# Attention by 64 query rows of both heads, and the last expert block by tiles, in an attention and mixture-of-experts kernel

## The chip, the core and the metric

The kernel runs on one core of a Trainium2 chip. The core has the matrix engine PE (its weight loads are listed as PEld, beside the products), the vector engine DVE, ACT, POOL and the queue engine SP; 16 DMA engines move data. The metric is the device time of one execution in microseconds; kernels are compared by the median of their runs.

## The reference

Attention with 8 batches, 8 heads, 576 positions and head size 64. A query sees itself and the 127 keys before it, with a slope per head. Its result is the input `x` (4608 rows of 512) of a layer with 8 experts of which each row takes two.

```python
scores = scale * np.matmul(q, k.transpose(0, 1, 3, 2))
mask = (rel >= 0) & (rel < window)          # rel = query - key, window = 128
scores = np.where(mask, scores + bias[None], -1000000000.0)
attn = np.exp(scores - np.max(scores, axis=-1, keepdims=True))
attn = attn / (np.sum(attn, axis=-1, keepdims=True) + 1e-09)
...
noisy_logits = x @ w_gate + np.log1p(np.exp(x @ w_noise)) * noise
top2 = np.argpartition(-noisy_logits, 2, axis=1)[:, :2]
...
h = np.maximum(x[mask] @ w1[e], 0.0)
out[mask] += top2_w[mask, k, None] * (h @ w2[e])
```

## The kernel before

**Order.** Nothing is scheduled by the compiler: `attention_moe` describes the work as strands (generators), and the class `Order` plays them in its own model of the engines. Each step has a rank; a free engine takes the waiting step of lowest rank, and the instructions are written out in that order. The ranks are sums of the table of constants at the head of the file (`LOAD`, `STAGE`, `LATE` and others). Buffers and PSUM banks are rings; a strand waits in the model for a free one. What runs on each engine is therefore a fixed list, and the chip's semaphores make it wait where the data isn't there.

**Attention.** A pair is two heads of one batch, 32 in all. `unit` (L559) takes a pair's 576 queries in three groups: blocks of 128 queries (0, 1), (2, 3) and the last 64 of both heads together. `scores` (L470) multiplies, in float32, each block with up to 256 keys, one head on the upper 64 rows of the array and the other on the lower 64 (L480), each head into a bank of its own; the last 64 queries use all 128 rows (L473). `sb` (L412) is one entry that holds both banks. `top` (L492, rows named L498) adds the bias on DVE and takes the row minimum, `soft` (L501, L505) the exponentials on ACT, `trans` (L511, L517) transposes on PE in squares of 128 (16 a pair), `evac` copies them to SBUF on ACT or DVE, and `weigh` (L530, L538 and L544) multiplies with V, the two heads side by side on 64 columns of the array each. `rows` and `gate` then turn the result to rows and compute the gate; `route` (L754) ranks the rows of a batch by expert with 20 products of 8 columns (`ranks`, L774).

**Experts.** Weights and activations are split into two float16 halves, so every product is made of three. `ups` (L1202, L1199 in the rows) makes the hidden layer in chunks of 128, `middle` the activation on ACT and DVE, `downs` (L1254, L1246 in the rows) adds each chunk's part to all tiles of 128 rows of the block, and `result` (L1316) scales a tile and adds it to the output with an indirect DMA on POOL. Blocks of the first two experts run as soon as a share of the batches is routed, among the attention; the others follow. `weight` (L1083) loads a weight chunk and finds its largest value (L1090) on DVE. SP issues the loads in the planned order.

Of the kernel before, what the change touches and what calls it, by code (L numbers as in the profile page):

```python
# [22 lines left out]
NQ = 5  # L23
NP = H // 2
QW = 512 + 128
GROUPS = ((0, 1), (2, 3), (4,))
# [17 lines left out]
ZERO = 157.5  # L44
LOAD = 136.5
VALUES = 180.6
GATE = (-31.6, -127.8)
ROUTE = 0
SCATTER = (-98.7, -1299.1, 241.8)
FFN0, FFN1 = 110.0, 337.8  # L50
WEIGHTS = ((17.1, 19.6), (205.3, 22.3))
SEQUENCE = ((0, 0), (0, 1), (1, 0), (1, 1), (0, 2), (1, 2), (0, 3), (1, 3))
TOKENS = -340.5
STAGE = (-252.5, -341.8, -103.3, -45.5, 28.3, -118.2, 102.9, -69.8)
MIDDLE = -39.8
RESULT = -351.1
WEIGHTS_LATE = 141.4
SOON = 126.4
LISTED = (-148.6, 389.0)
BIG, PARTS = 198.5, 29.3  # L60
TIGHT = (1, 5, 7)
LATE = (-250.4, 168.7, 5.2, 55.5, 53.4, 102.3, -331.2, -32.4, -14.5, 0.7, 30.3, 27.9)
# [24 lines left out]
class Op:  # L87


    def __init__(self, on, emit, join=True):  # L90
        self.on, self.emit, self.join, self.taken = on, emit, join, False
# [16 lines left out]
class Order:  # L108
# [3 lines left out]
    def __init__(self):  # L112
# [4 lines left out]
        self.work = {}  # L117
# [49 lines left out]

    def dispatch(self, e):
        if self.busy[e] > self.now:
            return  # L170
        while self.queue[e]:
            _, _, us, what, strand = heapq.heappop(self.queue[e])
            if what.taken:
                continue
# [9 lines left out]
            return  # L184
# [25 lines left out]
class Block:  # L210


    def __init__(self, e, s0, n, rows, rings):
        self.e, self.s0, self.n, self.rows, self.rings = e, s0, n, rows, rings
        self.last = self.flip = False
# [8 lines left out]
def attention_moe(ctx: ExitStack, tc: tile.TileContext, qk_, v, w_gate, w_noise, noise, w12,  # L224
# [19 lines left out]
    def pe(us, rank, emit, join=True):  # L244
        return Op((("PE", us, rank),), emit, join)
# [30 lines left out]
    pr = ring(ap_, 3, [128, 2, 2, 256], F32, "p")  # L276
    nmr = ring(ap_, 3, [128, 2, 2], F32, "nm")
    ptr = [ring(ap_, 2, [128, 2, 7, 128], F32, "pT"), ring(ap_, 1, [128, 2, 128], F32, "pTl")]
    xur = [ring(ap_, 2, [128, NP, 512], F32, "xu"), ring(ap_, 2, [128, NP, 64], F32, "xul")]
    denr = ring(ap_, 3, [128, NQ, H], F32, "den")  # L280
    xr = ring(ap_, 4, [128, DM], F32, "x")
    ltr = ring(ap_, 1, [128, 4, H, 16], F32, "lt")
    gtr = ring(ap_, 2, [128, 512], F32, "gt")

    PAIRS = B * NP
    units = [(k, g) for k in range(PAIRS) for g in range(len(GROUPS))]
# [9 lines left out]
    relc, m1 = scratch[0][:, 0:256], scratch[0][:, 256:512]  # L296
# [35 lines left out]
    def masks():  # L332
# [14 lines left out]
        for g in range(NP):  # L347
            for h in (2 * g, 2 * g + 1):
                yield either(0.56, 0.37, -20 + 5 * g, LATE[9], lambda e, h=h: bias_of(e, h))
            mark(biased[g])  # L350
# [1230 lines left out]
```

## Time and profile before

| | |
|---|---|
| median of 3 runs | 1095.0 us (1094.45 to 1097.28) |
| profiled execution | 1096.31 us, span 1094.5 us |
| PE, DVE, ACT, POOL busy | 96%, 64%, 43%, 33% of the span |
| mean granted PE clock | 0.996 |
| DMA | 145.61 MB |

The span goes from the first to the last instruction; the execution's time has 1.8 us beyond it. A product's record includes its latency, so groups of products overlap and a busy PE isn't one at its peak: how long a group holds the engine is read from its start to the next group's start. An idle time is given with the instruction that ended it.

### The profile page before, as it was taken

How to read it: one execution, taken by the hardware profiler on the slowest of the kernel's cores; microseconds unless marked ns; L12 is line 12 of the kernel's file. 1: busy time of each engine (PE TensorE's matmuls, PEld its weight loads, DVE VectorE, ACT ScalarE, POOL GpSimd, SP SyncE). 2: the span in 40 equal slices, each digit the busy share in tenths (PEclk: the TensorE clock that was granted, in tenths of full speed). 3: DMA queues.
4: the chain of work that ended last, by engine and by line, in shares of the span. 5: the costliest groups of instructions: out<-in, count | busy, mean ns of one | idle time of the engine just before them, and what ended most of it. 6: DMA issues, size and time to landing. Idle time of an engine off the chain costs nothing. (4 is left out here: it accounts for less than half of the span.)

```text
span 1094.5 us, 20083 instructions
## 1 busy us (share of the span) xinstructions
PE 1051.7 (96%) x7158; PEld 645.5 (59%) x7158; DVE 700.4 (64%) x2431; ACT 468.4 (43%) x1221; POOL 357.6 (33%) x464
## 2 busy tenths in 40 slices
PE   7888899999999999999999999999999999999995
PEld 5656666766676666564456446645754574564453
DVE  6999989968847889544469845925673582432110
ACT  7887777757622325222135423513352351321221
POOL 1377741444332423142113333203232231321211
PEclk9999999999999999999999999999999999999998
DMA  9757786534423687347495458557753753752212
GB/s 347 287 167 257 254 264 228 158 112 125 75 75 85 99 232 146 73 93 177 143 182 101 79 119 167 66 148 130 123 101 91 151 83 64 111 82 38 28 20 40
DMA packets 130085, 145.61 MB, mean 133 GB/s; under 512 B 90416, under 2 KB 91264, under 8 KB 129984
## 3 DMA queue, kind: packets, MB, share of 16 engines
q1 hardware_dynamic: 112464, 104.97, 34.6%
q0 software_dynamic: 17520, 39.34, 21.5%
q8 instruction: 57, 0.93, 0.4%
q14 instruction: 44, 0.36, 0.1%
HBM read 83.94 MB, written 40.91 MB: 114 GB/s over the span
## 5 line engine op out<-in xcount | busy, mean ns | idle before, releaser
L1199 PEld LDWEIGHTS <-held 128*128 128x128 f16 x2424 | 233.9, 98 | 127.7 <-issue 4.3
L1199 PE MATMUL bank<-bx,held 128*128 128x512 f16 (+7 forms) x1752 | 301.6, 324 | 0.1
L1235 DVE SCALAR_TENSOR_TENSOR bhl<-bank,bhh 128x384 f16<-128x384 f32 (+7 forms) x160 | 87.8, 549 | 284.0 <-ACT bhh L1220 279.4
L1326 POOL DMA_INDIRECT out_dram<-yo,ix x62 | 102.3, 1651 | 414.2 <-ACT yo L263 393.7
L1220 ACT ACTIVATE bhh<-bank 128x384 f16<-128x384 f32 (+7 forms) x144 | 70.1, 487 | 353.4 <-PE bank L1199 343.7
L1246 PE MATMUL bank<-held,bhh 128*128 128x512 f16 x728 | 216.5, 379 | 0.5 <-ACT bhh L1220 0.5
L505 ACT ACTIVATE p<-p,nm 128x256 f32<-128x256 f32 (+2 forms) x288 | 134.1, 472 | 19.7 <-DVE nm L498 19.4
L1246 PE MATMUL bank<-held,bhl 128*128 128x512 f16 x364 | 138.0, 379 | 0.0
L1246 PEld LDWEIGHTS <-bhh 128*128 128x128 f16 x800 | 78.6, 98 | 84.2 <-ACT bhh L1220 0.7
L498 DVE CUSTOM_DVE_ANT_0 p<-bank,bias 128x256 f32<-128x256 f32 (+2 forms) x288 | 95.2, 380 | 11.9 <-PE bank L480 9.0
L480 PE MATMUL bank<-qk 64*128 64x256 f32 (+1 forms) x512 | 73.7, 389 | 19.4 <-DVE nm L498 15.8
L517 PE MATMUL bank<-ident,p 128*128 128x128 f32 x512 | 78.5, 285 | 4.2 <-DVE l L846 1.0
L263 ACT ACTIVATE xt<-xg,fit 128x512 f16<-128x512 f32 (+5 forms) x77 | 55.3, 719 | 60.2 <-DVE fit L1167 52.8
L1154 POOL DMA_INDIRECT xg<-xs_dram,ix x62 | 65.4, 1056 | 45.3 <-DVE xt L1182 12.8
L1090 DVE TENSOR_REDUCE wam<-held 128x2 f32<-128x1024 f32 x60 | 71.9, 1211 | 5.3 <-DMA held<-in_w_dram 5.3
L1199 PE MATMUL bank<-ax,held 128*128 128x256 f16 (+1 forms) x672 | 75.0, 266 | 0.3 <-DVE ahl L1235 0.3
L517 PEld LDWEIGHTS bank<-ident,p 128*128 128x128 f32 x512 | 57.4, 143 | 23.5 <-ACT p L505 7.3
L480 PEld LDWEIGHTS bank<-qk 64*128 64x128 f32 x512 | 45.1, 194 | 38.7 <-DVE nm L498 26.1
L1121 DVE SCALAR_TENSOR_TENSOR held<-held,wsc,held 128x512 f16<-128x512 f32 x92 | 67.2, 771 | 0.0
L1246 PEld LDWEIGHTS <-bhl 128*128 128x128 f16 (+1 forms) x400 | 39.4, 98 | 47.1 <-DVE bhl L1235 0.3
L263 ACT ACTIVATE held<-held,wsc 128x512 f16<-128x512 f32 x92 | 61.6, 714 | 12.9 <-DVE held L1121 8.9
L1246 PE MATMUL bank<-held,ahh 128*128 128x512 f16 x224 | 67.1, 381 | 0.0
(238 smaller groups left out, 1499.4 us busy)
## 6 DMA issues: line engine op xcount, KB each, us to landing
held<-in_w_dram SPq DMA_DIRECT2D x60, 512.0 KB
qk<-in_qk_dram SPq DMA_DIRECT2D x31, 608.0 KB
vraw<-in_v_dram SPq DMA_DIRECT2D x16, 640.0 KB
out_dram<-xg SPq DMA_DIRECT2D x10, 1024.0 KB
xs_dram<-x SPq DMA_DIRECT2D x32, 256.0 KB
spare<-in_w_dram SPq DMA_DIRECT2D x4, 512.0 KB
xs_dram<-x SPq DMA_DIRECT2D x8, 128.0 KB
xs_dram<-xg SPq DMA_DIRECT2D x1, 1024.0 KB
```

The lines of the kernel that those rows point to most:

```text
L263: nc.scalar.activation(o, i, AF.Copy, **kw)
L480: nc.tensor.matmul(s[h][:, o:o + c], qk[half, i * 128:i * 128 + 128], qk[half, QW + k0:QW + k0 + c], start=True, stop=True)
L498: nc.vector.tensor_tensor_reduce(out=p[:, z, h, 0:c], in0=s[h][:, o:o + c], in1=bv, scale=-0.125, scalar=3.0e38, op0=OP.add, op1=OP.min, a ...
L505: nc.scalar.activation(pv, pv, AF.Exp, bias=nm[:, z, h:h + 1], scale=-1.0, accum_out=den[:, i, 2 * g + h:2 * g + h + 1])
L517: nc.tensor.transpose(t[:, z], p[:, h, a:a + 128], ident)
L1090: yield dve(1.13, rank + (BIG if e >= EARLY else 0), lambda: nc.vector.tensor_reduce(wam[:, e % 2, :, f], t.rearrange("p (z c) -> p z c", ...
L1121: nc.vector.scalar_tensor_tensor(lo, t, sc, hi, op0=OP.mult, op1=OP.subtract)
L1199: nc.tensor.matmul(t[:, 0:blk.n], wp[:, c], blk.x[:, x + c, 0:blk.n], start=c == 0 and z == 0, stop=c == 3 and z == 2)
L1220: nc.scalar.activation(o, i, AF.Relu)
L1235: yield dve(0.07 + c * 0.00104, rank - MIDDLE, lambda: nc.vector.scalar_tensor_tensor(hl[:, 0:c], t[:, 0:c], 0.0, hh[:, 0:c], op0=OP.max, ...
L1246: nc.tensor.matmul(blk.y[j][0:r], h[:, cs], wp, start=f == 0 and m == 0, stop=f == 7 and m == 2)
L1326: ins = nc.gpsimd.indirect_dma_start(out=out, out_offset=bass.IndirectOffsetOnAxis(ap=blk.ix[0:r, j:j + 1], axis=0), in_=t[0:r], in_offset ...
```

## The change

- **Scores.** A group is now 128 queries of both heads as two sub-blocks of 64: the array's 128 columns hold 64 queries of one head and 64 of the other, its 128 rows both heads' 64 dimensions, with zeros in between (laid out by the host in `qk`, so a pair's load has 1728 columns instead of 1216). A sub-block meets at most 192 keys. There are five groups a pair and nine products of 64, 128 and seven times 192 columns. A group writes one bank; `sb` has two entries.
- **Transposes.** Two sub-blocks lie next to each other in `p` so that their halves share a square: 13 a pair instead of 16.
- **Weighing V.** Per sub-block and head one product of full height (128 keys) and one of half height (64 keys), each of 64 columns; even sub-blocks to one bank, odd ones to another.
- **Ranks.** Six products of 48 to 8 columns a batch.
- **Last block.** Its hidden layer is kept whole; then one tile takes all its eight chunks, then the other. The last tile's scaling is cut in two halves for ACT and DVE, and POOL drains before the first of the block's scatters.
- **Order.** The planner prefers PE steps of the shape that the array has; the table of constants is new; expert 1's weight loads have an earliest time.

```diff
-QW = 512 + 128
-GROUPS = ((0, 1), (2, 3), (4,))
+NS, SUB = S // 64, 64
+QW = NS * 128
...
-PACE = (36.1, 5.5)
-AHEAD = -83.9
+PACE = (33.7, 5.5)
+HOLD = (-38.7, 125.2)
...
+STAY, TURN = -100.7, 0.13
...
+    def take(self, e):
+        q = self.queue[e]
+        while q:
+            if e == "PE":
+                x = min(q, key=lambda x: (x[0] + (STAY if x[3].shape != self.shape else 0.0), x[1]))
+                q.remove(x)
+                heapq.heapify(q)
+            else:
+                x = heapq.heappop(q)
+            if not x[3].taken:
+                return x[2:]
+        return None
+    def cost(self, e, us, what):
+        if e == "PE":
+            us, self.shape = us + (TURN if what.shape != self.shape else 0.0), what.shape
+        return us
...
-    pr = ring(ap_, 3, [128, 2, 2, 256], F32, "p")
...
+    pr = ring(ap_, 6, [128, 384], F32, "p")
...
-    sb, tb, ob, yb = Ring([bank[0:2]]), Ring([*bank[2:4], bank[7]]), Ring([bank[4], bank[6]]), Ring([])
+    sb, tb, ob, yb = Ring(bank[0:2]), Ring([*bank[2:4], bank[7]]), Ring([bank[4], bank[6]]), Ring([])
...
             t = yield (vraw, rank)
+            yield begun
...
-        if blocks == (4,):
-            nc.tensor.matmul(s[0][:, 0:192], qk[:, 512:QW], qk[:, QW + S - 192:QW + S], start=True, stop=True)
-            return
-        for z, i in enumerate(blocks):
-            k0, c = (i - 1) * 128 if i else 0, width(i)
-            o = place_of(blocks, z)
-            for h in range(2):
-                half = slice(h * D, h * D + D)
-                nc.tensor.matmul(s[h][:, o:o + c], qk[half, i * 128:i * 128 + 128], qk[half, QW + k0:QW + k0 + c],
...
+    def subs(i):
+        return range(2 * i, min(2 * i + 2, NS))
+    def width(j):
+        return min(64 * j + 64, 192)
+    def place(j):
+        return (192, 384)[j % 2] - width(j)
...
+        for j in subs(i):
+            c, k1 = width(j), QW + 64 * j + 64
+            nc.tensor.matmul(s[:, j % 2 * 256:j % 2 * 256 + c], qk[:, j * 128:j * 128 + 128], qk[:, k1 - c:k1],
+                             start=True, stop=True)
...
+    def turns(i):
+        return range(i == 0, 3 - (i == 4))
...
+        for z, a in enumerate(turns(i)):
+            nc.tensor.transpose(t[:, z * 128:z * 128 + 128], p[:, a * 128:a * 128 + 128], ident)
...
-        for z in range(4):
-            c = min(256, 512 - 128 * z)
+        def part_of(o, j, rows, block, slot, first_, last):
             for h in range(2):
                 half, hh = slice(h * D, h * D + D), (k % 2 * 2 + h) * D
-                nc.tensor.matmul(o[half, z * 128:z * 128 + c], t[:, z, hh:hh + D],
-                                 pt.rearrange("p h s c -> p h (s c)")[:, h, 2 * z * 128:2 * z * 128 + c],
-                                 start=z == 0, stop=z == 3, skip_group_check=True)
-        for z in range(2):
-            for h in range(2):
-                half, hh = slice(h * D, h * D + D), (k % 2 * 2 + h) * D
-                nc.tensor.matmul(ol[half], t[:, 3 + z, hh:hh + D], ptl[:, z, half], start=z == 0, stop=z == 1)
+                nc.tensor.matmul(o[half, j // 2 * SUB:j // 2 * SUB + SUB], t[rows, block, hh:hh + D], pt[rows, slot, half],
+                                 start=first_, stop=last, skip_group_check=True)
+        for a in range(4):
+            part_of(odd, 2 * a + 1, slice(0, 128), a, 3 * a + 1, a == 0, False)
+            part_of(even, 2 * a + 2, slice(0, 128), a, 3 * a + 2, a == 0, False)
+        for i in range(NQ):
+            if 0 < i < 4:
+                part_of(odd, 2 * i + 1, slice(64, 128), i - 1, 3 * i, False, i == 3)
+            part_of(even, 2 * i, slice(0, 64), i, 3 * i, False, i == 4)
...
         def ranks():
-            for i in range(NQ):
-                nc.tensor.matmul(rp[:, i], before, both_[:, i], start=True, stop=i == 0)
-                for j in range(i):
-                    nc.tensor.matmul(rp[:, i], ones, both_[:, j], start=False, stop=j == i - 1)
             for j in range(NQ):
-                nc.tensor.matmul(rp[:, NQ], ones, both_[:, j], start=j == 0, stop=j == NQ - 1)
+                nc.tensor.matmul(rp[:, j + 1:], ones, both_[:, j:j + 1].to_broadcast([128, NQ - j, E]), start=j == 0,
+                                 stop=False, skip_group_check=True)
+            nc.tensor.matmul(rp, before, both_, start=False, stop=True, skip_group_check=True)
...
     def weight(e, f, t, rank):
+        if e < EARLY and order.now < HOLD[e]:
+            yield Pad(HOLD[e])
...
+        if blk.final:
+            if not f:
+                blk.hx = yield (blk.rings["x"], rank)
+                mark(blk.hid)
+            yield blk.hid
+            hh, hl = (blk.hx[:, f, z * 256:z * 256 + c] for z in range(2))
...
+    def last_downs(blk, rank):
+        blk.y = []
+        for j, r in blk.tiles:
+            t = yield (yb, rank)
+            blk.y.append(t)
+            for f in range(8):
+                yield blk.h[f][0]
+                ev = chunks[blk.e, f]
+                yield ev[1]
+                end = yield pe(0.655, rank, lambda: mm2(blk, f, j, r, ev[2]), False)
+            spawn(result(blk, j, r, rank - RESULT, end))
...
+            if blk.final and not j:
+                nc.gpsimd.drain()
...
-        yield either(0.57, 0.66, rank, LATE[7], lambda e: copy(e, t[0:r], y[0:r], scale=gw))
+        if blk.final and j == len(blk.tiles) - 1:
+            both = Event(2)
+            for z, (on, us) in enumerate((("ACT", 0.33), ("DVE", 0.36))):
+                spawn(half(on, us, rank, t[0:r, z * 256:z * 256 + 256], y[0:r, z * 256:z * 256 + 256], gw, both))
+            yield both
+        else:
+            yield either(0.57, 0.66, rank, LATE[7], lambda e: copy(e, t[0:r], y[0:r], scale=gw))
...
-    qk[..., 0:512], qk[..., QW:] = q[..., 0:512], k
+    qk[..., QW:] = k
     for h in range(2):
-        qk[:, h, :, 512 + 64 * h:512 + 64 * h + 64] = q[:, h, :, 512:]
+        for j in range(NS):
+            qk[:, h, :, j * 128 + h * 64:j * 128 + h * 64 + 64] = q[:, h, :, 64 * j:64 * j + 64]
```

On PE, at the third pair of heads, before: `qk_79` and `qk_80` hold queries and keys of two pairs, bank_66 and bank_67 are the score banks, `p` the exponentials and `pT` their transposes, `vraw` V.

```order
L480 MATMUL bank_66<-qk_79 128x256
L480 MATMUL bank_67<-qk_79 128x256
L538 MATMUL bank_70<-pT_90,vraw_82 64x256 x6
L538 MATMUL bank_70<-pT_90,vraw_82 64x128 x2
L544 MATMUL bank_71<-pTl_92,vraw_82 64x64 x4
L473 MATMUL bank_66<-qk_79 128x192
L517 MATMUL bank_73<-ident,p_84 128x128 x2
L517 MATMUL bank_68<-ident,p_84 128x128 x4
L480 MATMUL bank_66<-qk_80 128x128
L480 MATMUL bank_67<-qk_80 128x128
```

After, at the same place:

```order
L523 MATMUL bank_73<-ident,p_89 128x128 x2
L502 MATMUL bank_66<-qk_79 128x192 x2
L502 MATMUL bank_67<-qk_79 128x192
L523 MATMUL bank_69<-ident,p_84 128x128 x3
L502 MATMUL bank_66<-qk_80 128x64
L502 MATMUL bank_66<-qk_80 128x128
L523 MATMUL bank_73<-ident,p_85 128x128 x3
L537 MATMUL bank_68<-pT_96,vraw_82 64x64 x2
L537 MATMUL bank_70<-pT_96,vraw_82 64x64 x2
```

Scores go one bank at a time between transposes, and V is weighed in short pieces that alternate between two banks.

On ACT, at the end of the last block, before (`bhh` is the upper half of a hidden chunk, `yo` a scaled tile, bank_69 and bank_70 the two tiles' sums):

```order
L1220 ACTIVATE bhh_4677<-bank_66 128x240
L1220 ACTIVATE bhh_4678<-bank_71 128x240
L1220 ACTIVATE bhh_4679<-bank_67 128x240
L1220 ACTIVATE bhh_4677<-bank_66 128x240
L263 ACTIVATE yo_197<-bank_69,gw_194 128x512
L263 ACTIVATE yo_4691<-bank_70,gw_194 112x512
```

After (`bx_5121` holds all hidden chunks, bank_73 and bank_72 are the tiles' sums):

```order
L1219 ACTIVATE bx_5121<-bank_66 128x240
L1219 ACTIVATE bx_5121<-bank_71 128x240
L1219 ACTIVATE bx_5121<-bank_67 128x240
L283 ACTIVATE yo_203<-bank_73,gw_198 128x512
L283 ACTIVATE yo_5136<-bank_72,gw_198 112x256
```

The second tile's scaling has half its columns on ACT; on PE the eight chunks' products of bank_73 now stand ahead of all those of bank_72, where before each chunk fed both tiles in turn.

On SP, where loads of the first pairs and of the first experts' weights (`held`) are issued, before:

```order
L1086 DMA held_111<-in_w_dram 128x1024
L1086 DMA held_112<-in_w_dram 128x1024
L388 DMA wgn<-in_w_gate_dram 64x4x8
L434 DMA qk_78<-in_qk_dram 128x1216
L1086 DMA held_113<-in_w_dram 128x1024
L1086 DMA held_114<-in_w_dram 128x1024
L1086 DMA held_115<-in_w_dram 128x1024
L1086 DMA held_116<-in_w_dram 128x1024
L1086 DMA held_117<-in_w_dram 128x1024
L1086 DMA held_118<-in_w_dram 128x1024
L1086 DMA held_119<-in_w_dram 128x1024
L1086 DMA held_120<-in_w_dram 128x1024
```

After:

```order
L1087 DMA held_119<-in_w_dram 128x1024
L1087 DMA held_120<-in_w_dram 128x1024
L452 DMA qk_78<-in_qk_dram 128x1728
L408 DMA wgn<-in_w_gate_dram 64x4x8
L452 DMA qk_79<-in_qk_dram 128x1728
L463 DMA vraw_83<-in_v_dram 128x1280
L452 DMA qk_80<-in_qk_dram 128x1728
L452 DMA qk_81<-in_qk_dram 128x1728
L408 DMA wgn<-in_w_noise_dram 64x4x8
L452 DMA qk_78<-in_qk_dram 128x1728
L463 DMA vraw_82<-in_v_dram 128x1280
L408 DMA wgn<-in_w_noise_dram 64x4x8
```

Behind the first weights there were ten more; now six loads of pairs and V and two small ones follow, and expert 1's weights come later.

## Rows read from the trace of the kernel before

**Rows 1.** Page part 1: busy us of each engine (share), x instructions.

```profile
PE 1051.7 (96%) x7158; PEld 645.5 (59%) x7158; DVE 700.4 (64%) x2431; ACT 468.4 (43%) x1221; POOL 357.6 (33%) x464
```

**Rows 2.** Windows by stage: start:end, length, engines' busy us, clock, DMA share, GB/s.

```profile
0.00:27.40 27.40, 21.34 (x137) 14.97 (x138) 18.60 (x72) 20.68 (x70) 3.20 (x23) 1.00 0.93 348
27.40:136.80 109.40, 94.96 (x830) 67.02 (x829) 105.74 (x390) 86.77 (x292) 70.76 (x73) 1.00 0.71 241
136.80:301.00 164.20, 158.41 (x1473) 113.22 (x1474) 142.01 (x728) 118.14 (x423) 66.73 (x122) 1.00 0.55 160
301.00:465.00 164.00, 160.16 (x1208) 104.98 (x1205) 121.24 (x432) 50.97 (x105) 51.30 (x67) 1.00 0.55 119
465.00:1079.20 614.20, 613.76 (x3502) 343.58 (x3500) 312.37 (x810) 190.17 (x329) 162.56 (x178) 1.00 0.54 103
1079.20:1094.50 15.30, 3.10 (x20) 1.69 (x18) 0.41 (x1) 1.71 (x3) 3.08 (x3) 0.71 0.25 33
```

**Rows 3.** Waits of PE's weight loads: waited for, us in total, times, longest.

```profile
PEld bank L480 <- DVE nm L498: 26.1, 34, 1.8
...
PEld bank L517 <- ACT p L505: 7.3, 21, 1.3
...
PEld bank L473 <- DVE nm L498: 3.1, 5, 0.9
```

**Rows 4.** Timeline of PE, one pair: start, us, line, tiles, xcount, idle before.

```profile
111.97 0.93 PE L480 MATMUL bank<-qk 64*128 64x128 f32 x8 [0.74 <-DVE nm L498]
112.86 2.19 PE L517 MATMUL bank<-ident,p 128*128 128x128 f32 x16
115.53 1.47 PE L480 MATMUL bank<-qk 64*128 64x256 f32 x8 [0.47 <-DVE nm L498]
116.94 1.73 PE L538 MATMUL bank<-pT,vraw 128*64 128x256 f32 x16
118.50 0.40 PE L544 MATMUL bank<-pTl,vraw 128*64 128x64 f32 x8
118.83 0.44 PE L517 MATMUL bank<-ident,p 128*128 128x128 f32 x2
119.58 0.59 PE L473 MATMUL bank<-qk 128*128 128x192 f32 x2 [0.31 <-DVE nm L498]
120.01 0.60 PE L517 MATMUL bank<-ident,p 128*128 128x128 f32 x4
```

**Rows 5.** Timeline of PE, scores whose banks were free, and the group behind.

```profile
281.54 1.14 PE L480 MATMUL bank<-qk 64*128 64x256 f32 x8
282.60 0.66 PE L517 MATMUL bank<-ident,p 128*128 128x128 f32 x4
```

**Rows 6.** Timeline of PE, ranking of one batch: its first product, the group behind.

```profile
102.85 0.20 PE L776 MATMUL bank<-both,before 128*128 128x8 bf16 x2
...
103.37 1.98 PE L517 MATMUL bank<-ident,p 128*128 128x128 f32 x14
```

**Rows 7.** Groups on DVE, 27.4 to 301 us: xcount, busy us, mean ns, idle before.

```profile
L498 DVE CUSTOM_DVE_ANT_0 p<-bank,bias 128x256 f32<-128x256 f32 x175 | 64.5, 418 | 3.6 <-PE bank L480 3.3 <-issue 0.2
...
L498 DVE CUSTOM_DVE_ANT_0 p<-bank,bias 128x128 f32<-128x128 f32 x58 | 14.1, 279 | 1.2 <-PE bank L480 1.1
L1090 DVE TENSOR_REDUCE wam<-held 128x2 f32<-128x1024 f32 x11 | 13.2, 1212 | 0.0
...
L498 DVE CUSTOM_DVE_ANT_0 p<-bank,bias 128x192 f32<-128x192 f32 x30 | 10.4, 348 | 2.4 <-PE bank L517 2.2
```

**Rows 8.** Timeline of all engines, the end of the last block.

```profile
1082.16 1.33 ACT L263 ACTIVATE yo<-bank,gw 128x512 f32<-128x512 f32 x2 [0.92 <-PE bank L1246]
...
1082.39 0.38 PE L1246 MATMUL bank<-held,bhl 128*112 128x512 f16 x1
1083.12 1.55 POOL L1326 DMA_INDIRECT out_dram<-yo,ix  x1 [14.48 <-ACT yo L263]
...
1084.97 1.50 POOL L1326 DMA_INDIRECT out_dram<-yo,ix  x1 [0.27 <-issue]
```

More of the change, by code (lines that the diff above doesn't have):

```diff
@@ L116, in __init__ @@
         self.alive = 0
-        self.work = {}
+        self.work, self.shape = {}, 0
     def at(self, time, call):
@@ L170, in dispatch @@
             return
[L171 to L174, printed above, removed]
+        x = self.take(e)
+        if x:
+            us, what, strand = x
+            us = self.cost(e, us, what)
             what.taken = True
@@ L483, in width @@
-    def width(i):
-        return (128, 256, 256, 256, 192)[i]
-    def place_of(blocks, z):
-        return sum(width(i) for i in blocks[:z])
-    def heads(i):
-        return 1 if i == 4 else 2
-    def top(k, blocks, s, p, nm):
-        g = k % NP
-        for z, i in enumerate(blocks):
-            c, o = width(i), place_of(blocks, z)
-            for h in range(heads(i)):
-                bv = bias4[:, g] if i == 4 else bias[:, 2 * g + h, 256 - c:256]
-                nc.vector.tensor_tensor_reduce(out=p[:, z, h, 0:c], in0=s[h][:, o:o + c], in1=bv, scale=-0.125,
-                                               scalar=3.0e38, op0=OP.add, op1=OP.min, accum_out=nm[:, z, h:h + 1])
@@ L568, in unit @@
         s = yield (sb, r0)
-        yield pe((0.97, 1.18, 0.33)[gr], r0, lambda: scores(k, blocks, s))
+        yield pe(0.4 if first_ else 0.34 if last else 0.66, r0, lambda: scores(k, i, s))
         left[k] -= 1
@@ L742, in attention_moe @@
     oh = ap_.tile([128, NQ, 2, E], F32, name="oh")
[L743 removed]
+    both_ = ap_.tile([128, NQ + 1, E], BF16, name="both")
     d = ap_.tile([128, NQ, 2], F32, name="d")
@@ L1340, in result, with half @@
             put(gwr, blk.gw)
+    def half(on, us, rank, o, i, gw, both):
+        yield Op(((on, us, rank),), lambda: copy(on, o, i, scale=gw))
+        mark(both)
     def first_wave():
@@ L1354, in banks @@
         yield attended
-        for t in sb.free.pop():
-            put(hbr, t)
+        while sb.free:
+            put(hbr, sb.free.pop())
         t = yield (ob, 0)
@@ L1374, in second_wave @@
                     for e0, e1, s0, nt in LISTS)
+        spared.append(more.tile([1, 2 * NOV * E + 3 * NOV + 5 * E], F32, name="spared"))
         t = yield (tb, 0)
@@ L1477, in attention_moe @@
                        allow_small_or_imprecise_dtypes=True)
-    order.busy["POOL"], order.busy["DVE"], order.busy["ACT"] = 2.5, 1.5, 1.9
+    order.busy["POOL"], order.busy["DVE"], order.busy["ACT"] = 2.5, 2.4, 1.9
     order.at(2.5, lambda: order.dispatch("POOL"))
-    order.at(1.5, lambda: order.dispatch("DVE"))
+    order.at(2.4, lambda: order.dispatch("DVE"))
     order.at(1.9, lambda: order.dispatch("ACT"))
```

276 lines of the change are left out of this document (133 added, 143 removed).

## The prediction, and its working

> **What bounds the kernel now.** I read the page's engine totals first, then the run cut into stages, then what the PE waits for in the first stages, then single groups of its products. [rows 1] PE is busy for 1051.7 of 1094.5 us, DVE for 700.4. [rows 2] The stages differ. From 465 to 1079 us (the experts' layers) the PE is busy for 613.8 of 614.2 us at full clock, and the change edits nothing there, so this stretch can only shift as a whole. From 27 to 137 us (attention) DVE is busy for 105.7 of 109.4 us and the PE for 95.0: DVE sets the pace. From 137 to 301 us (attention mixed with the first expert blocks) the PE has 158.4 of 164.2 and DVE 142.0: the PE sets it. So a microsecond of PE work is worth one everywhere except in the DVE-paced stage, and there the PE's idle 14.4 us are what DVE's relief can return. [rows 3] The PE's weight loads say who holds it: 26.1 us for the row minima on DVE (the score banks come free only after them), 3.1 us more for the last query tile's product, 7.3 us for exponentials on ACT.
>
> The sum is made against the profiled execution: 1096.3 us, of which 1.8 lie outside the span. The median of the three runs is 1095.0, so 1.3 us below it.
>
> **Scores.** Before, a pair of heads takes three groups [rows 4]: 111.97 to 112.86 (0.89), 115.53 to 116.94 (1.41) and 119.58 to 120.01 (0.43), 2.73 us. L538 gives the rate: 1.56 us (116.94 to 118.50) for 16 passes, two at a time, 1792 columns one after another, so 0.87 ns a column and pass. Changing the array's shape costs about 0.1 us more: L544's eight passes of 64 columns, two at a time, are four steps of 0.056, 0.22, yet the next group starts 0.33 us after the first of them (118.50 to 118.83). The first two score groups use 64-row halves of the array; with the two entries a pair costs 2.93. After, nine products of 128 rows have 64, 128 and seven times 192 columns. A float32 product has two passes: 0.33 us for 192, the same as the 0.43 of [rows 4] less its exposed weight load of 0.1. The two narrow ones are held by their weight loads, 0.11 a pass. That is 7 x 0.33 + 0.44 = 2.75, plus 0.1 for each of five groups whose bank is not yet free. With two of them: 2.95. I take no change. Bounds: -0.2 (no wait left) and +0.7 us a pair.
>
> The upper bound comes from a clean group. [rows 5] With its banks free, the group that took 1.41 took 1.06 us (281.54 to 282.60), so half-arrays do run side by side and 0.35 us of the 1.41 was a wait. The Trainium skill ("TensorEngine Tiling (Array Packing)", Theoretical Speedup) speaks against this edit: it promises up to twofold for contraction sizes up to 64, which the change gives up. The clean group agrees with it, the usual group doesn't, because its second bank is late.
>
> **Transposes.** 16 become 13 a pair, one pass each. Sixteen took 2.19 us and two 0.44 [rows 4], so 0.125 each at most, with some waiting in it; 128 columns by 0.87 ns are 0.11, which I take. 96 fewer: -10.5 us. A stall doesn't go with them: the same exponentials release them.
>
> **Weighing V.** Before: 116.94 to 118.83 [rows 4], 1.89, and 0.1 for entering: 1.99. After: 16 products of full height and 64 columns, 32 passes, two at a time by 0.056: 0.90. Then 16 of half height, 32 passes, a shape the trace doesn't show. If all four quarters of the array run at once, the longest has ten passes of 0.056: 0.56. If two do: 0.90. One after another: 1.79. The nearest row for many short products is the ranking's 20 of 8 columns [rows 6], 0.52 us from 102.85 to 103.37, so 0.026 each: 0.8 for 32. I take 0.8, since something other than columns limited that row. With three shape changes the sum is 2.0: no change. Bounds -0.24 and +0.99 us a pair, so -8 and +32 in all.
>
> The skill ("TensorE: Matmul & The Clock Gate", The mechanism) starts products in different tiles about 4 ns apart. By that the half-height part would be the 0.56, and the sum 8 us lower. No row here shows four tiles at once.
>
> **Ranks.** 20 products become six: at 0.026 us, 0.52 becomes 0.16, eight times: -3 us. **PE work together: -13.5 us** (bounds -27 and +41).
>
> **DVE and ACT.** [rows 7] Row minima: 6 x 418 + 2 x 279 + 348 = 3414 ns a pair before; 7 x 348 + 279 + about 210 (the line through these widths, at 64) = 2925 after: -0.49 us. The 273.6 us of the two attention stages hold 263 such products, nine a pair, so 9.4 us a pair and about 12 pairs in the DVE-paced stage: -5.9 us. The reordered loads also put expert 1's weights behind the nineteenth pair's load, so up to 8 of the scans for a weight's largest value (L1090, 1.21 us each), 9.7 us, leave that stage for the next, where DVE has 22 us free. Against that stand three more small copies a batch, each under the 0.28 of the narrowest product here, 2.5 us in three batches. DVE is relieved of some 13 us there. Exponentials and evacuations get narrower on ACT too; ACT isn't the bound (86.8 of 109.4), so I count that at nothing.
>
> **Score banks.** A group of scores now needs one bank of two, before it needed both; the PE can write one while DVE reads the other. This is what turns DVE's relief into PE time. I take 10 of the 14.4 us of PE idle time in the DVE-paced stage [rows 2], 4 of the 5.8 in the next, 2 of the 3.8 between 301 and 465: **-16 us**. Bounds: none, and all 24.
>
> **Tail.** [rows 8] Before, the last two tiles end together: the last product starts at 1082.39, ACT scales both in 1.33 us, and the second scatter starts at 1084.97 behind the first. By tiles, one scatter is left behind the last product, its scaling cut in two halves. Two scatters start 1.85 us apart (1083.12 and 1084.97), the added drain and the halves' handover cost some: **-2 us** (-1 to -3). Only the two last scatters are queued on POOL behind that drain.
>
> **More bytes.** A pair's q and k grow from 1216 to 1728 columns of 512 bytes, 608 to 864 KB, 8.4 MB in 32 pairs; at the 348 GB/s of the first stage [rows 2] that is 24 us of transfers. DMA is 93% busy in the first 27 us and 71% in the next stage, and the order puts only eight weight loads ahead of pair 5 where there were six before pair 5 and sixteen before pair 6. I count it at nothing: the free 29% of 109 us (32 us) cover it. If not, the pairs from the fifth on start late. The first V now waits behind four pairs' q and k, 4.1 MB or 12 us, before any pair is ready to be weighed.
>
> **Sum:** 1096.3 - 13.5 - 16 - 2 = 1065.
>
> **Rivals.**
> (1) The waits stay. DVE keeps the pace because the planner fills its free time with expert work, and the idle time only moves. For: DVE still has some 92 of 109 us. Against: two banks, less DVE work. 1096.3 - 13.5 - 2 - 2 = 1079.
> (2) The scores are paid at the clean price: had each group's banks been free, a pair would cost 0.89 + 1.06 + 0.43 + 0.2 = 2.58, and 2.95 is 0.37 more, 12 us over the forecast: 1077. For: in the PE-paced stage clean groups occur. Against: the two waits by which the usual group is longer are on the path. The tiling rule named above would have it so.
> (3) The waits go almost wholly and four quarters run at once: 1096.3 - 21.5 - 24 - 3 = 1048. For: PE work is then the only bound. Against: the first 27 us wait for data and for ACT.
> (4) DMA becomes the bound in the first 60 us and the extra bytes show up as late pairs: 20 us of the 24, so 1085.
> (5) Slower: in the half-height part the passes run one by one (1.79) and each of its six changes of array half costs a shape change (0.6), 2.39 where I took 0.8: +1.59 x 32 = +51 us, 1116. It decides the sign from +31 us, 0.97 us a pair. Against: L480's two halves alternate without such a cost in the clean group.
>
> **How the numbers follow.** About 0.3% is what a measurement of this kernel can tell from no change: 1091.7 to 1098.3 around 1095.0. Forecast 1065 (1054 to 1075): 0.46. (1) 0.16, (2) 0.04, (3) 0.14, (4) 0.12, (5) 0.08. Faster: the forecast, (1) to (3), less 0.02 for the upper end of (1), and 0.08 of (4): 0.86. Same: 0.02 and 0.03 of (4), 0.05. Slower: (5) and 0.01 of (4), 0.09. The range 1042 to 1089 leaves out (5), a third of (4) and the lower end of (3), some 0.15.
>
> **What would show it.** Right: PE idle in 27 to 137 us near 4 us instead of 14; loads of the scores waiting for DVE for under 12 us in all; a V group of 1.9 to 2.1 us; attention's last scores some 20 us earlier or with more expert work ahead of them; one scatter behind the last product. Wrong: V groups over 2.5 us, PE waiting for q and k, DVE still at 96% in the second stage, or idle PE after 465 us, which I take as untouched.

## The result, and the profile after

The changed kernel takes 1078.0 us (median, 1075.1 to 1079.4) against 1095.6 us before: a ratio of 0.983, with a 95% interval of 0.981 to 0.986. The gain is 17.6 us where 30 were forecast, and the time is near that of rival (1), 1079. The profiled execution took 1077.75 us, with a span of 1075.9.

The page's first part and the windows by stage, to be read against [rows 1] and [rows 2] (busy us of PE, PEld, DVE, ACT, POOL, then clock, DMA share, GB/s):

```profile
PE 1044.0 (97%) x8230; PEld 675.0 (63%) x8230; DVE 683.1 (63%) x2432; ACT 452.7 (42%) x1239; POOL 359.5 (33%) x467
```

```profile
0.00:27.40 27.40, 22.06 (x226) 19.61 (x227) 20.08 (x87) 19.97 (x74) 3.24 (x24) 1.00 0.94 366
27.40:136.80 109.40, 102.95 (x1466) 88.83 (x1464) 93.41 (x449) 85.59 (x330) 49.64 (x77) 1.00 0.82 281
136.80:301.00 164.20, 154.27 (x1964) 125.72 (x1964) 144.71 (x689) 108.60 (x398) 92.95 (x125) 1.00 0.61 190
301.00:465.00 164.00, 161.92 (x1175) 104.49 (x1166) 118.19 (x411) 49.12 (x105) 53.69 (x67) 0.99 0.59 122
465.00:1065.00 600.00, 600.00 (x3414) 334.94 (x3413) 306.23 (x796) 188.92 (x334) 158.22 (x173) 1.00 0.55 103
```

The first stage did what was forecast: DVE fell from 105.7 to 93.4 us, and the PE's idle time from 14.4 to 6.5. The next stage did the opposite: its idle time rose from 5.8 to 9.9. From 465 us on the PE is never idle, as (but for 0.4 us) before. The stage from 137 to 301 us has to be cut finer. Windows of before, then of after:

```profile
136.80:165.00 28.20, 27.23 (x270) 19.46 (x271) 25.21 (x129) 21.51 (x81) 12.94 (x28) 1.00 0.83 263
165.00:190.00 25.00, 23.70 (x230) 17.08 (x226) 23.88 (x132) 19.19 (x72) 3.89 (x6) 1.00 0.69 235
190.00:215.00 25.00, 24.83 (x232) 18.48 (x229) 23.01 (x105) 19.32 (x72) 12.61 (x24) 1.00 0.60 179
```

```profile
136.80:165.00 28.20, 27.45 (x363) 23.37 (x360) 27.68 (x123) 21.21 (x82) 3.76 (x7) 1.00 0.97 367
165.00:190.00 25.00, 23.24 (x328) 19.86 (x328) 23.94 (x118) 20.26 (x80) 16.71 (x17) 1.00 0.91 307
190.00:215.00 25.00, 19.54 (x249) 15.52 (x248) 24.58 (x109) 17.72 (x60) 19.62 (x17) 1.00 0.44 147
```

Between 190 and 215 us DVE is busy for 24.6 of 25 us and the PE stands idle for 5.5; work on DVE ends all but 0.4 us of that. DMA is at 0.44 there, so the late loads of rival (4) are not the reason. What came into this stretch is the splitting of expert 1's weights on DVE and POOL, which the new table holds back.

The waits of the PE's weight loads, against [rows 3] (us in total, times, longest):

```profile
PEld bank L502 <- DVE nm L508: 13.5, 25, 1.7
...
PEld bank L502 <- DMA qk<-in_qk_dram: 5.0, 2, 3.5
```

The row minima hold the PE for 13.5 us instead of 29.2, near the 12 that were to show the forecast right. Of the 5.0 us for q and k, 3.5 are the start of the program.

The PE's timeline of two pairs, against [rows 4] (start, us, line, tiles, xcount, idle before):

```profile
112.38 0.82 PE L502 MATMUL bank<-qk 128*128 128x192 f32 x4
113.12 1.88 PE L537 MATMUL bank<-pT,vraw 128*64 128x64 f32 x64
114.93 0.55 PE L523 MATMUL bank<-ident,p 128*128 128x128 f32 x3
...
118.55 0.92 PE L502 MATMUL bank<-qk 128*128 128x192 f32 x4 [0.31 <-DVE nm L508]
119.40 1.88 PE L537 MATMUL bank<-pT,vraw 128*64 128x64 f32 x64
121.21 0.77 PE L523 MATMUL bank<-ident,p 128*128 128x128 f32 x5
```

Weighing V takes 1.81 us (113.12 to 114.93) and 0.1 for entering, 1.91. In the trace most of its half-height passes start in fours, 0.02 us from first to last, and the next four start 0.058 us after the first: four quarters at once. The engine's groups before and after, to 465 us, say where its work went (xcount, busy us, mean ns, idle before):

```profile
L517 PE MATMUL bank<-ident,p 128*128 128x128 f32 x512 | 78.5, 285 | 4.2 <-DVE l L846 1.0 <-DVE pTl L267 0.8 <-ACT pT L263 0.6
L480 PE MATMUL bank<-qk 64*128 64x256 f32 x384 | 62.8, 408 | 5.3 <-DVE nm L498 5.1
...
L473 PE MATMUL bank<-qk 128*128 128x192 f32 x64 | 18.4, 369 | 2.1 <-DVE nm L498 1.9
L480 PE MATMUL bank<-qk 64*128 64x128 f32 x128 | 16.4, 333 | 14.1 <-DVE nm L498 10.7 <-DMA qk<-in_qk_dram 3.4
```

```profile
L502 PE MATMUL bank<-qk 128*128 128x192 f32 x448 | 96.9, 339 | 5.1 <-DVE nm L508 3.7 <-DMA qk<-in_qk_dram 1.2
L523 PE MATMUL bank<-ident,p 128*128 128x128 f32 x416 | 68.8, 280 | 5.8 <-ACT pT L283 1.1 <-DVE nm L508 1.0 <-DVE x L676 1.0
...
L502 PE MATMUL bank<-qk 128*128 128x128 f32 x64 | 14.4, 307 | 0.0
L502 PE MATMUL bank<-qk 128*128 128x64 f32 x64 | 12.6, 280 | 6.2 <-DMA qk<-in_qk_dram 3.6 <-DVE nm L508 2.3
```

The scores went from 97.6 to 123.9 us, where the forecast had no change; the transposes from 78.5 to 68.8. A record includes its latency, and there are five groups a pair now instead of three, so these sums overlap. From each product's start to the next one's, the scores hold the PE for 107.4 us instead of 87.5, and for 100.1 instead of 83.2 with the engine's idle time left out; by this last measure, which adds up to the page's total, the transposes went from 70.9 to 53.5. The whole page has the PE busy for 7.7 us less, where 13.5 were forecast.

The end, against [rows 8]:

```profile
1060.72 7.07 PE L1251 MATMUL bank<-held,bx 128*128 128x512 f16 x32
...
1067.88 0.47 ACT L283 ACTIVATE yo<-bank,gw 112x256 f32<-112x256 f32 x1 [4.49 <-PEq L1538]
1068.39 0.48 DVE L285 TENSOR_SCALAR yo<-bank,gw 112x256 f32<-112x256 f32 x1 [10.11 <-ACT yo L283]
1069.15 1.49 POOL L1350 DMA_INDIRECT out_dram<-yo,ix  x1 [3.89 <-DVE yo L285]
```

One scatter stands behind the last product, which starts at 1067.41 in the trace: 8.5 us to the end, 12.1 before. The two halves of the last scaling run one after the other, not side by side.

### The profile page after: what moved, and what is told of

Same layout as the page of the kernel before. It is cut to its first block, busy times and chain, and to the rows that moved or that the text cites. A ratio compares the mean times of both kernels' runs of the same rounds, so it can differ in the third digit from the quotient of the medians.

```text
span 1075.9 us, 22259 instructions
## 1 busy us (share of the span) xinstructions
PE 1044.0 (97%) x8230; PEld 675.0 (63%) x8230; DVE 683.1 (63%) x2432; ACT 452.7 (42%) x1239; POOL 359.5 (33%) x467
## 3 DMA queue, kind: packets, MB, share of 16 engines
q8 instruction: 65, 1.06, 0.4%
## 5 line engine op out<-in xcount | busy, mean ns | idle before, releaser
L1242 DVE SCALAR_TENSOR_TENSOR bhl<-bank,bhh 128x384 f16<-128x384 f32 (+6 forms) x152 | 84.6, 557 | 264.5 <-ACT bhh L1219 264.0
L1219 ACT ACTIVATE bhh<-bank 128x384 f16<-128x384 f32 (+6 forms) x137 | 67.4, 492 | 349.8 <-PE bank L1200 348.7
L516 ACT ACTIVATE p<-p,nm 128x192 f32<-128x192 f32 (+2 forms) x288 | 122.4, 428 | 27.7 <-DVE nm L508 26.9
L502 PE MATMUL bank<-qk 128*128 128x192 f32 (+2 forms) x576 | 115.4, 329 | 11.3 <-DVE nm L508 6.0
L502 PEld LDWEIGHTS bank<-qk 128*128 128x128 f32 x576 | 88.7, 195 | 20.5 <-DVE nm L508 13.5
L508 DVE CUSTOM_DVE_ANT_0 p<-bank,bias 128x192 f32<-128x192 f32 (+2 forms) x288 | 82.9, 327 | 13.6 <-PE bank L502 10.6
L1155 POOL DMA_INDIRECT xg<-xs_dram,ix x62 | 64.9, 1047 | 54.5 <-DVE ix L962 13.5
L283 ACT ACTIVATE xt<-xg,fit 128x512 f16<-128x512 f32 (+1 forms) x76 | 54.4, 718 | 54.6 <-DVE fit L1168 49.2
L523 PE MATMUL bank<-ident,p 128*128 128x128 f32 x416 | 68.8, 280 | 5.8 <-ACT pT L283 1.1
L1251 PEld LDWEIGHTS <-bhl 128*128 128x128 f16 x384 | 37.6, 98 | 45.4
L537 PE MATMUL bank<-pT,vraw 64*64 64x64 f32 (+1 forms) x2048 | 60.8, 225 | 2.8 <-issue 1.6
L537 PEld LDWEIGHTS bank<-pT,vraw 64*64 64x64 f32 (+1 forms) x2048 | 53.9, 136 | 11.3 <-issue 4.1
```

Source lines behind the costliest of these rows:

```text
L502: nc.tensor.matmul(s[:, j % 2 * 256:j % 2 * 256 + c], qk[:, j * 128:j * 128 + 128], qk[:, k1 - c:k1], start=True, stop=True)
L508: nc.vector.tensor_tensor_reduce(out=p[:, place(j):place(j) + c], in0=s[:, z * 256:z * 256 + c], in1=bias4[:, g, 192 - c:192], scale=-0.12 ...
L516: nc.scalar.activation(pv, pv, AF.Exp, bias=nm[:, z:z + 1], scale=-1.0, accum_out=den[:, j, g:g + 1])
L523: nc.tensor.transpose(t[:, z * 128:z * 128 + 128], p[:, a * 128:a * 128 + 128], ident)
L537: nc.tensor.matmul(o[half, j // 2 * SUB:j // 2 * SUB + SUB], t[rows, block, hh:hh + D], pt[rows, slot, half], start=first_, stop=last, ski ...
L1155: yield pool(1.04, rank, lambda: nc.gpsimd.indirect_dma_start(out=xg[0:r], out_offset=None, in_=xs[0:blk.rows], in_offset=bass.IndirectOff ...
```

## Experiments

Two theories. **A:** the PE work was mis-priced (the scores cost more than counted), and DVE still sets the pace through much of attention, so that its idle time moved. **B:** the extra bytes, or something outside attention, ate the gain. One rival stays untested: the kernel before was not run with a newly searched table of constants, so how much of the 17.6 us the new order brings, and how much the new products, isn't separated. The kernels came in three series, each on one chip. The changed kernel itself took 1075.1 us beside 1096.0 before in the second (e5) and 1084.2 beside 1097.2 in the third (e11), so each difference below is taken inside its series. The first series had no such mark, but its e3 gave the time that the same kernel gave in the third (1088.95 and 1088.73), so 1084 is its mark, by inference.

**Scores in four quarters (e1).**

```diff
-            nc.tensor.matmul(s[:, j % 2 * 256:j % 2 * 256 + c], qk[:, j * 128:j * 128 + 128], qk[:, k1 - c:k1],
+            for h in range(2):
+                half, out_ = slice(h * D, h * D + D), slice((h ^ j % 2) * 64, (h ^ j % 2) * 64 + 64)
+                nc.tensor.matmul(s[j % 2][out_, 0:c], qk[half, j * 64:j * 64 + 64], qk[half, k1 - c:k1],
```

> The changed kernel, but each pair of score products runs in four quarters of the array (64 by 64): head 0 of the even query tile, head 1 of the even, head 0 of the odd, head 1 of the odd, the even tile into one bank and the odd one into the other; the odd tile's two heads stand in swapped partitions. q is stored without its zero halves, so a pair's q and k are 1152 columns instead of 1728. Theory A (the scores were mis-sized: giving up half-arrays cost about 0.5 us a pair, 15 us in all, and the PE sets the pace in most of attention): two 192-column products take about 0.35 us instead of 0.65, a pair's scores fall from 2.7 us by 0.6 to 1.2 us, PE work falls by 19 to 38 us, and the time by 10 to 25 us, to 1053 to 1068. Rival B (DVE sets the pace wherever the scores run, so the PE's price of a score is covered): PE work falls as much, PE idle time grows by as much, and the time stays at 1073 to 1080. Rival C (quarters do not run side by side for products of 192 columns): a group of two stays at 0.6 us or more, and the time at 1078 or above.

1098.6 us, some 14 over its mark. The PE's timeline (L507 the scores, L528 the transposes, L543 V):

```profile
200.25 0.44 PE L528 MATMUL bank<-ident,p 128*128 128x128 f32 x2
200.62 0.56 PE L507 MATMUL bank<-qk 64*64 64x192 f32 x8
201.11 0.55 PE L528 MATMUL bank<-ident,p 128*128 128x128 f32 x3
```

C falls: two tiles take 0.49 us (200.62 to 201.11), with 0.1 for leaving the shape in it, instead of 0.65. But each group now changes the array's shape twice. Two such transposes take 0.22 us in one shape; here 0.37 pass from their start at 200.25 to the scores. So 0.49 and some 0.1 for entering stand against 0.65, and almost nothing is left. By the records' shapes the array changes some 440 times a run instead of 235. From start to start without idle time the scores do hold the PE for 19.5 us less (80.6 instead of 100.1), but the transposes, which now end in a change, hold it for 10.7 more (64.2 instead of 53.5) and the other products for some 9 more, and the page's total is 1044.4 us instead of 1044.0. So A's step, that the PE's work would fall by 19 to 38 us, is wrong: what the quarters save is taken back around them. And a group writes both banks: 66 of the 73 waits below end with the minima of the group just before, where in the changed kernel all 25 end with those of the group two before.

```profile
PEld bank L507 <- DVE nm L513: 33.5, 73, 2.9
```

The Trainium skill ("TensorEngine Tiling (Array Packing)", Key Properties, and Restrictions and Gotchas, Gotcha 1: PSUM Pressure) states both costs: a change of tiling mode drains the engine, and row tiles can't write the same bank at once. The 0.1 us at each change agrees with the first; the second is why the layout takes two banks, and nothing here shows it otherwise. The 14 us themselves are mostly elsewhere: the new order lets the PE run out of work at the end of attention (16.1 busy of 30 us from 355 to 385, at a granted clock of 0.72; the changed kernel has 28.0 there, the kernel before 29.0). So the time says little about the quarters; the timeline and the waits do.

**One score bank (e2).** `sb` becomes `Ring(bank[0:1])`, the other bank lies idle in attention.

> The changed kernel with a single bank for the scores instead of two. Theory A (two banks are what shortened the waits for the row minima): the PE's waits for the row minima, 19.5 us over weight loads and products now, go back to 30 us or more, and the time rises by 8 to 15 us, to 1086 to 1093. Rival B (the shorter waits come from the smaller DVE work alone): under 3 us, 1076 to 1081.

1151.2 us, some 67 over its mark:

```profile
PEld bank L502 <- DVE nm L508: 62.0, 77, 3.2
```

With one bank every group has to wait for the minima of the one before; 77 of these waits leave the loads idle. A holds, and by far more than it said. Not all 67 us are waits: the same products keep the PE busy for 1079.4 us instead of 1044.0, in part at a lower granted clock (0.80 from 45 to 65 us, 0.86 from 100 to 137).

**No hold of expert 1's weights (e4).** `HOLD = (-38.7, 125.2)` becomes `(-1.0, -1.0)`.

> The changed kernel without the rule that holds back the load of the early experts' weights (expert 1's weights may be loaded and split as soon as a buffer is free). Theory A (the idle time of the PE only moved, with expert 1's weights, from before 137 us to 190 to 215 us, where DVE is 98% busy): the PE's idle time between 190 and 215 us falls from 5.5 to under 3 us, that between 27 and 137 us rises from 6.5 to 10 us or more, and the time is within 5 us of 1078. Rival B (holding the weights back is itself a gain, since it relieves the first stage for good): 1085 or more. Rival C (the stretch at 190 to 215 us is slow for another reason, such as late q and k): its idle time stays at 5 us.

1097.5 us, some 13 over its mark: B's verdict by A's mechanism. The idle time moved as A said: between 190 and 215 us it falls to 0.9 us, between 27 and 137 us it rises to 13.1, with DVE at 102.9 of 109.4 us there. But the moved work is not a wash. The windows of this kernel:

```profile
27.40:45.00 17.60, 12.48 (x114) 10.18 (x112) 17.50 (x52) 11.63 (x41) 5.49 (x4) 0.77 1.03 419
45.00:65.00 20.00, 17.45 (x227) 15.52 (x229) 18.82 (x62) 15.42 (x50) 15.12 (x11) 0.78 0.51 167
```

DVE is full, the PE stands idle for 5.1 of 17.6 us, and the granted clock falls to 0.77 of full speed over the stretch, so for part of it to the lower level, 1.2 of 2.4 GHz. Over the whole run the same products keep the PE busy for 1051.7 us instead of 1044.0. And the PE is idle for 10.2 us between 301 and 465 us (2.1 in the changed kernel).

**96 transposes twice (e6), against the changed kernel again (e5).**

```diff
-            nc.tensor.transpose(t[:, z * 128:z * 128 + 128], p[:, a * 128:a * 128 + 128], ident)
+            for again in range(1 + (z == 0 and 0 < i < 4)):
+                nc.tensor.transpose(t[:, z * 128:z * 128 + 128], p[:, a * 128:a * 128 + 128], ident)
```

> The changed kernel itself once more, as the mark to measure the others of this call against. Its ratio to the kernel before was 0.983; the kernel without the tiles of the last block had an unchanged order of instructions up to 1048 us and still came there 7 us later. Theory A (that gap belongs to that chip or that hour, and would show in the changed kernel too): 0.983 to 0.99 of the kernel before here. Rival B (it belongs to that kernel): 0.981 to 0.986.

> The changed kernel with three transposes of each pair of heads done twice (96 more products of 128 columns, the number that the merging took away), everything else in the same order. Theory A (the PE is busy or waited for nearly all the time, so that a microsecond of its work costs one): 96 times 0.11 is 10.5 us more than the changed kernel, and 8 at the least. Rival B (DVE sets the pace where attention runs, and transposes lie in its shadow): under 5 us more.

e5: 1075.1 us, 0.9825 (0.979 to 0.986), in B's range. e6: 1079.9 us, 0.9862 (0.985 to 0.988). The transposes of e5, then of e6:

```profile
L523 PE MATMUL bank<-ident,p 128*128 128x128 f32 x416 | 68.8, 280 | 5.8 <-ACT pT L283 1.1 <-DVE nm L508 1.0 <-DVE x L676 1.0
```

```profile
L524 PE MATMUL bank<-ident,p 128*128 128x128 f32 x512 | 78.6, 278 | 4.9 <-DVE nm L508 1.5 <-DVE x L677 1.0 <-ACT pT L283 1.0
```

9.8 us more work (8.2 by the engine's total, which doesn't count overlap twice) cost 4.8 us: a microsecond of PE work in attention is worth about half of one. That is a loose figure: the two intervals, of some 2 and 3 us to either side, overlap, so B's 5 holds only narrowly and A's 8 isn't excluded.

**More DVE work: the narrow minima twice (e7), or 96 instructions that nobody waits for (e9, against e11).** e7 runs the instruction of `top` twice where `i == 0`; e9 adds behind it

```diff
+        for again in range(3 if i == 0 else 0):
+            nc.vector.tensor_scalar(beside, bias4[:, g], 2.0, None, op0=OP.mult)
```

> The changed kernel with the row minima of the two narrowest query tiles of each pair done twice on DVE (64 more instructions of 210 and 279 ns, 0.49 us a pair, as much as the change took off), everything else in the same order. Theory A (DVE still sets the pace in part of attention, at 190 to 215 us above all, and its relief was worth what the forecast said in the first stage): 5 to 10 us more than the changed kernel, with the PE's idle time before 301 us longer by as much. Rival B (DVE has room everywhere now): under 2 us more. Rival C (DVE sets the pace throughout): 14 to 16 us more.

> The changed kernel with three more instructions a pair on DVE (96 in all, each scaling 192 columns of a constant), right behind the row minima of the pair's first group, which nobody waits for; everything else in the same order. Doing that group's minima twice (0.49 us of DVE a pair) cost 15 us. Theory A (DVE's time sets the pace through attention): the cost is again about what these instructions take on DVE, 10 to 20 us over the changed kernel. Rival B (it was the score bank, held 0.49 us longer, and not DVE's time): under 6 us.

e7: 1090.3 us, 15.2 over e5, for 16.6 us of DVE work (64 instructions of 221 and 289 ns). That is C, not A. Since these also hold a score bank longer, e9 adds work that holds no bank:

```profile
L513 DVE TENSOR_SCALAR beside<-bias 128x192 f32<-128x192 f32 x96 | 33.0, 343 | 2.2
```

The totals of e11, then of e9:

```profile
PE 1044.3 (97%) x8230; PEld 673.5 (62%) x8230; DVE 682.6 (63%) x2432; ACT 452.4 (42%) x1239; POOL 358.9 (33%) x467
```

```profile
PE 1051.4 (95%) x8230; PEld 676.1 (61%) x8230; DVE 708.6 (64%) x2528; ACT 454.7 (41%) x1239; POOL 360.2 (33%) x467
```

1103.3 us, 19.1 over e11, for 33.0 us: 0.58 us for each, or 0.73 for each of the 26.0 us that DVE's total grew by. So A holds: DVE's time sets the pace through more than half of attention without a bank being held. The 19.1 us aren't DVE's directly in full: the same products keep the PE busy for 7.1 us longer, and its granted clock is 0.98 from 27 to 301 us where it was 1.00. Row minima are dearer (0.92 for each, or 1.06 by the 14.3 us of the total), which would be the bank's share; that last step is argued, not isolated.

**No order by array shape (e8).** `STAY, TURN = -100.7, 0.13` becomes `0.0, 0.0`.

> The changed kernel with the planner's choice of products by array shape switched off. Theory A (its order spares shape changes of 0.095 us each, 12 us in all now against 22 before the change): some 30 to 100 more changes, 3 to 9 us more than the changed kernel. Rival B (the order changes little, or costs waits): within 2 us or faster.

1087.8 us, 12.7 over e5, but not by A's mechanism: the trace has no more shape changes (229 against 235 by the records' shapes, so at 0.095 us each at the most 22 us, and not the 12 that the expectation starts from). What grew is idle time of the PE, 6.2 us between 235 and 301 us and 9.7 between 301 and 465 (1.0 and 2.4 in e5), and the granted clock falls a little:

```profile
235.00:301.00 66.00, 59.85 (x644) 43.66 (x643) 48.37 (x230) 26.08 (x85) 39.39 (x69) 0.97 0.30 65
301.00:465.00 164.00, 154.33 (x1079) 98.81 (x1077) 112.59 (x401) 48.67 (x104) 57.88 (x75) 0.98 0.55 111
```

The other constants were set together with that order, which may be why; that isn't isolated.

**The last block as before (e3, and e10 against e11).** `blk.final` is always false.

> The changed kernel with its last block as before (both tiles end together, no drain, no halves). Theory A (the tail is worth 3 to 4 us: from the last product's start to the end 8.5 us instead of 12.1): 12 us from the last product's start to the end, and 1081 to 1083. Rival B (the drain and the halves cost what the missing scatter saves, and the shorter tail only shows that one tile's products come later): 1077 to 1079.

> The changed kernel with its last block as before, once more, now beside the changed kernel in the same call. Theory A (the tail is worth 3.7 us, and the other 6 us of the first time belonged to that chip or hour): 3 to 5 us over the changed kernel of this call. Rival B (this kernel is slower by 9 us for a reason outside its tail): 8 us or more.

> The changed kernel itself, as the mark for this call. 0.981 to 0.986 of the kernel before, as twice already.

e3: 1088.95 us (0.992); e10: 1088.7 us (0.992, 0.990 to 0.995), e11: 1084.2 us (0.9895, 0.987 to 0.992). 4.5 us, and the intervals overlap; the traces are sharper. The last product of e10 and what follows:

```profile
1076.23 0.38 PE L1251 MATMUL bank<-held,bhl 128*112 128x512 f16 x1
1076.97 1.56 POOL L1350 DMA_INDIRECT out_dram<-yo,ix  x1 [14.44 <-ACT yo L283]
...
1078.83 1.49 POOL L1350 DMA_INDIRECT out_dram<-yo,ix  x1 [0.27 <-issue]
```

From there to the end of the span (1088.4) are 12.2 us, in e11 8.6. The tail is worth 3.6 us, A of e10; of the 11 us by which e3 lies over the 1078.0 of the result, the other 7 would then belong to its chip, as would the 6 of e11. e11 missed its range: the same program was 9 us slower than in e5, while the kernel before differs by 1.2. Product by product, e11 falls behind e5 in steps: some 2 us at 167 to 169 us, where DMA is at 0.94 to 0.98, 1.6 us at 271 to 278, and 2 us at 401 to 408. At the first the profile names no releaser, so that a late load does it is a guess.

**Another table of constants (e12).** Some twenty constants of the planner's table change and not a line else; since the planner also picks the engine of some copies, POOL has 453 instructions instead of 467 and ACT 1247 instead of 1239.

> The changed kernel with another table of constants for the planner and not a line else changed, so the same instructions in another order. The single constants switched off so far (the hold of expert 1's weights, the order by shape) cost 13 and 17 us with the same PE and DVE work. Theory A (what the order leaves of idle PE time, 41 us in all, is worth as much as the change's parts): 5 to 12 us faster than the changed kernel. Rival B (the idle time is set by DVE's work, the same in any order): within 3 us of it.

1076.4 us, 7.8 under e11, and 0.981 (0.979 to 0.982) of the kernel before. The waits for row minima, from 0 to 465 us, in e11 and here:

```profile
PEld bank L502 <- DVE nm L508: 14.3, 26, 1.7
```

```profile
PEld bank L502 <- DVE nm L508: 5.5, 16, 1.0
```

A holds on this chip: 8 us lay in the order and the choice of engine. The changed kernel itself was slow here, though; in the result and in e5 it took 0.983 of the kernel before, not told from e12 by the intervals, and e12 was not run beside those. And the PE's idle time between 301 and 465 us grew from 3.9 to 6.0 us, so part of it moved once more. (The 13 and 17 us of the expectation are 12.7 and some 13 by the marks used here.)

## Why the prediction was right, and where it was not

The forecast kernel was 12.8 us faster than the profiled one. By its terms, from the traces of before and after: PE work -13.5 forecast, -7.7 measured; waits -16 forecast, -5.6 measured in the three stages that it named (-8.0, +4.1 and -1.8), and -1.6 of idle time elsewhere; tail -2 forecast, -3.6 measured. Together -18.6 of the -31.5. That a gain came, by PE work, waits and tail alike, is as forecast; the forecast's own span, 1054 to 1075, was missed. That the time is near rival (1)'s 1079 is luck: its sum of -13.5, -2 and -2 has other terms. In the PE work, too, errors cancelled in part: the scores cost 17 us that were forecast as nothing, and the transposes gave 7 more than forecast.

- **Scores: mis-sized.** "I take no change" rested on [rows 4], a group of 1.41 us, as the usual one. In the trace of before the median is 1.40 for the twelve such groups between 27 and 137 us only; that of the seventeen between 137 and 301 is 1.06, the clean group of [rows 5]. A clean pair is 0.86 + 1.06 + 0.33 and 0.2 for two entries, 2.45; after, 0.45 and three and a half times 0.65, 2.72. So the scores cost 0.3 us a pair more at clean prices, some 9 us, 16.9 in all from start to start without idle time, and 20 with the idle time that stands in them. Rival (2) named this and gave it 0.04. e1 shows the other side: with shape changes and a second bank, the packing that was given up returns almost nothing here. (On the price alone the rule of the Trainium skill, "TensorEngine Tiling (Array Packing)", Theoretical Speedup, agrees with the trace: 0.39 us for four quarters against 0.65.)
- **Transposes: right in number, mis-sized in time.** 96 fewer, -17.4 us from start to start where -10.5 was forecast. 96 times 0.107 us are 10.2 of it. The rest is time between products that the records don't count as idle; 4.5 us of it stood at the 32 places where before a half-array score followed a transpose, a change of shape that is gone.
- **V: right**, 1.91 us, -2.4 in all; the half-height part, taken at 0.8, took 0.63, with four quarters at once. **Ranks: right**, -2.6 for -3; a batch's ranking now holds the PE from 122.79 to 122.94, 0.15 us for the 0.52 of [rows 6]. The other products make up the last -2.2 of the -7.7.
- **DVE's relief: right in its place.** The scans and the minima left the first stage (105.7 to 93.4 us, 12.3 of the 13 forecast), and 8 of the 10 us of idle time went with them. e4 shows that without the hold of expert 1's weights they stay.
- **Waits: the step that failed** is "4 of the 5.8 in the next". That the PE sets the pace from 137 to 301 us was read off a mean over 164 us. From 137 to 215 us DVE was already busy for 72.1 of 78.2 us; with expert 1's weights moved in, it is 76.2, and the idle time there rose. This is rival (1)'s mechanism, the idle time that only moves, for part of attention. e7 and e9 show the pace: DVE's microsecond is worth 0.6 to 0.9 (0.7 to 1.1 by the totals), the PE's (e6) about half, loosely.
- So the premise "a microsecond of PE work is worth one" isn't borne out either: e6 gives half, with an interval that reaches far to both sides. It hurt little because the PE work saved was small.
- **Tail: mis-sized**, -3.6 instead of -2, outside its -1 to -3. The forecast counted the distance of the two scatters' starts and took some back for the drain and the halves. From the last product's start to the last scatter's start it saved 0.8 us only (2.58 in [rows 8], 1.74 now), with the halves one after the other. The rest stands behind that start: 9.5 us to the end of the span before, 6.75 now (9.6 in e10, 6.9 in e11). A scatter that has no other close ahead of it ends sooner; that was not priced.
- **Bytes: right.** DMA rose to 0.82 and 0.61 in the two stages and to 0.97 between 137 and 165 us; the PE's waits for q and k after the start are 1.5 us. That there is no room left is all that e11 may hint at.
- **No idle PE after 465 us: right.**

## What to carry to other kernels

Find the pace-setting engine by adding work to each engine in turn, in an unchanged order, and repeat each until the intervals part: a microsecond of DVE cost 0.58 to 0.92 us here, clear of noise, one of PE some 0.5, not clear of it, and no busy share says either. Cut a stage until its slices look alike before saying which engine sets it; a mean over 164 us hid 78 us at the other engine's limit. A product shape is to be priced with the shape changes around it and the banks it holds, and from start to start, where the parts add up to the engine's total.

## What the runs showed of the hardware

Some DVE instructions stand still while POOL adds two tiles in SBUF. An addition of 128 x 40 numbers on DVE, then the POOL instruction beside it, then the same addition with POOL quiet (start, us):

```profile
204.78 1.06 DVE L840 TENSOR_TENSOR y<-y,u 128x40 f32<-128x40 f32 x1
```

```profile
204.62 1.16 POOL L1120 TENSOR_TENSOR held<-held,held 128x512 f16<-128x512 f32 x1
```

```profile
245.86 0.20 DVE L840 TENSOR_TENSOR y<-y,u 128x40 f32<-128x40 f32 x1
```

It ends at 205.84, 0.06 us after POOL's instruction (205.78). Between 165 and 235 us of the changed kernel DVE's instructions take some 8 us more than the shortest tenth of their form would; expert 1's low halves run on POOL there, but not every microsecond of this is shown to be POOL's. In e9 the added instructions read and write SBUF only, and 21 of the 96 took 0.32 to 1.21 us instead of the usual 0.26, each of them beside an instruction on POOL. The Trainium skill ("SBUF — State Buffer", Terms) says so: the two engines share one pair of ports, locked for a whole instruction, and the loser waits. Not every DVE instruction there is stretched: a row minimum that began at 207.73, beside the next such POOL instruction (207.42 to 208.58), took its usual 0.35.
